# Shorter zero matmuls before the first scores, and moved words, in the opening table of an attention-and-MLP kernel

## The chip, the core and the metric

The kernel runs on one core of a Trainium2 chip. The core has five engines that work at the same time, each through its own list of instructions in order: TensorE (PE; its weight loads, PEld, overlap its matmuls), VectorE (DVE), ScalarE (ACT), GpSimd (POOL) and SyncE (SP). Engines wait for each other through semaphores. Transfers (DMAs) are issued by an engine, here mostly by GpSimd and SyncE, and land later.

The metric is the time of one execution on the device in microseconds (us). Before the change the median of three runs is 321.03 us (321.01 to 321.31).

## What is computed

Causal attention with a forget gate for 8 batches x 8 heads, 576 positions, head size 64, and then a two-layer MLP with a tanh-approximated gelu:

```python
scores = scale * np.matmul(q, k.transpose(0, 1, 3, 2))
cum = np.cumsum(np.log(np.clip(f, 0.0001, 1.0)), axis=-1)
decay = cum[:, :, :, None] - cum[:, :, None, :]
scores = np.where(causal, -1000000000.0, scores + decay)
attn = softmax(scores)
x = np.matmul(attn, v)          # as (4608, 512): tokens x (head, d)
h = x @ w_in                    # 512 -> 2048
g = 0.5 * h * (1.0 + np.tanh(c * (h + 0.044715 * h * h * h)))
out = g @ w_out                 # 2048 -> 512
```

## The kernel before

Attention is worked in 16 quads of four heads. Quad i loads its queries and keys (q_c, k_c), VectorE transposes them into qT and kT, TensorE makes the scores in rounds into PSUM (ps_s), ScalarE takes the exponential into pt, GpSimd or VectorE masks the diagonal blocks, and TensorE multiplies pt with the weighted values vw (line 341 or 355) and with the gate's weights alone for the denominators. VectorE divides and writes xT, the MLP's input. The MLP works in nine chunks of 512 tokens: the first product into ps_h (lines 403 and 439), the gelu on ScalarE into gT, and the second product (lines 619 and, for chunk 0, 692).

Nothing is scheduled by a planner. The order is written by hand in the tables of words FRONT, SECOND, STEADY, FLUSH and LAST. `run` reads a table word by word and emits the instructions of each word; every engine keeps that order in its own list. So moving a word matters for an engine only if it passes another word with instructions on that same engine, or on its queue of transfers.

The words that the change and the prediction touch:

- `B.n.w`: n matmuls of zeros, w columns wide, on TensorE (line 258, `keep_busy`); they wait for nothing but the zeros. `BK.i.n`: n such matmuls of 512 columns that read quad i's transposed keys (line 264).
- `S.i.r`: round r of the scores of quad i, four heads, into two PSUM pairs, followed by two exponentials (lines 285 and 293). `H.i.r.g`: the same for two of the four heads, one pair and one exponential. There are two such pairs (pool psS), handed out in turn, also to `I`, `J` and `v`.
- `M` and `m`: masks by GpSimd (line 299) or by a product with a triangle on VectorE (line 329). `tr`: copies of the triangle into the two tiles `causal`, three copies on ScalarE (lines 740 and 741); `UT` makes the triangle on GpSimd.
- `D`: denominators (line 341 or 355). `V`, `v`: the product with the values, `v` into a pair of psS (ps_o).
- `TK.i`, `TQ.i`: transposes of keys and queries of quad i on VectorE (line 216). `LK.i`, `LQ.i`: their loads, issued by GpSimd (line 209).
- `LP.t`: values of batch 0, a block of 128 positions t, issued by GpSimd; LP.4 is the last block, half as long. `WI.c`, `WO.c`: blocks of the weights w_in and w_out, also issued by GpSimd (lines 198 and 202).
- `CE.n`: the gate's weights, on ScalarE (line 754). `w.0`, `cl`: small copies on ScalarE. `X`: a dummy exponential that has the table loaded ahead.
- `j.0.g.n`, `J.0.g`: n steps, or all, of the first MLP product for half of chunk 0 (line 439), with the gelu behind; `I`: the same for a whole chunk (line 403).
- `F.c.n`: n steps of the second product of chunk c; for chunk 0 (line 692) a step is one matmul of 128 columns of gT against 512 columns. `f.c.n`: the same steps, each as four matmuls of 32 columns side by side.

Of the kernel before, what the change touches and what calls it, by code (L numbers as in the profile page):

```python
# [16 lines left out]
def kernel(  # L17
# [12 lines left out]
    B, H, S, D = q.shape  # L30
# [38 lines left out]
    ON_ACT = ()  # L69

    FRONT = """
        B.1.128 B.1.512 B.1.256 SC B.8.512 B.1.256 B.1.512 B.1.128 LP.0 LP.1 CT B.2.512 WI.1 B.1.256 TK.0 B.1.128 B.1.128 BK.0.2 WI.0 LP.4
        BK.0.1 B.1.512 CE.0 TQ.0 B.1.512 CE.1 LP.3 B.1.512 BK.0.1 S.0.0 B.1.128 B.1.128 LP.2 TK.1 M.0.0 w.0 WI.5 BK.0.1 B.3.512 WI.2 H.0.2.1
        WI.3 B.1.128 TQ.1 BK.0.1 B.1.128 B.1.128 B.1.256 B.1.128 BK.1.1 B.1.512 H.0.1.0 WI.4 D.0.0 vw.0.0 vw.1.0 H.0.2.0 B.2.512 BK.1.1
        B.1.128 H.1.0.1 H.1.0.0 M.1.0 B.1.128 B.1.512 B.1.128 B.1.512 B.1.128 V.0.1.0 H.1.2.0 H.0.1.1 V.0.0.0 H.0.3.0 D.1.0 V.1.1.0 j.0.0.4
        M.0.1 UT LQ.2 WI.7 V.1.0.0 H.0.3.1 H.1.3.1 j.0.0.4 j.0.0.8 H.1.1.0 vw.0.1 WI.6 H.1.1.1 RJ.0.0 M.0.3 D.0.1 LK.2 WO.1 WO.0 j.0.1.8
        VW.1.1 H.1.2.1 tr H.1.3.0 M.1.3 V.0.1.1 V.0.0.1 J.0.2 j.0.1.8 M.1.1 D.1.1 V.1.0.1 V.1.1.1 GJ.0.1 W.1 TQ.2 J.0.3 J.1.1 GJ.0.0 J.1.3
        J.1.0 U.0 WO.2 J.1.2 LK.3 WO.3 LQ.3 LC.1.0 PW.2.1 PW.2.2 F.0.3 LC.1.3 f.0.2 LC.1.4 LC.1.1 LC.1.2 TK.2 f.0.1 LK.4 LQ.4 f.0.1 S.2.0
        F.0.5 TK.3 m.2.0 F.0.5 S.2.2 F.0.2 f.0.5 TQ.3 f.0.2 S.2.1 f.0.3 LV.2.1 F.0.6 S.3.0 F.0.2 m.2.1 vw.2 cl.2 F.0.2 f.0.1 LV.2.0 X M.2.2
        D.2 M.3.0 LQ.5 f.0.1 S.3.1 VW.3 f.0.2 V.2.0 LK.5 TQ.4 TK.4 f.0.4 S.3.2 LV.3.1 LQ.6 f.0.1 m.3.1 f.0.3 LK.6 V.2.1 M.3.2 f.0.3 S.4.1  # L80
        f.0.1 F.0.5 VW.4 TQ.5 F.0.1 X H.4.2.0 H.4.2.1 D.3 f.0.1 cl.3 H.4.0.0 H.4.0.1 V.3.1 v.3.0 vw.5 U.1 f.0.2 m.4.2.2 I.1.2 I.1.1 UW.2.4
        TK.6 I.1.0 CL.5 U.2 m.4.2.3 I.1.3 I.1.5 TQ.6 U.3 TK.5 I.1.4 G.0 I.1.6 M.4.1 I.1.7 F.1.1 G.1.1.2 cl.4 F.1.5 LV.3.0 F.1.5 S.5.0 F.1.5
        M.5.0 F.1.7 m.4.0 F.1.2 UW.2.3 F.1.2 LK.8 F.1.7 LK.7 D.4 S.5.1 F.1.17 LQ.8 F.1.1 S.5.2 M.5.2.3 M.5.2.2 f.1.2 V.4.0 f.1.1 M.5.1 f.1.8
        LQ.7@m.3.1 f.1.1 V.4.1 S.6.0 M.6.0 f.1.4 D.5 f.1.10 S.6.1 f.1.1 M.6.1 f.1.2 V.5.1 vw.6 F.1.4 CL.6 F.1.5 S.6.2 m.6.2.3 V.5.0 f.1.4
        m.6.2.2 f.1.3
    """

    SECOND = """
        Y F.-1.99 T.0.1 T.0.2 LB.2.0 T.0.3 T.0.4 LB.2.1 I.0.0 LB.2.2 E.0.2.2 I.0.1 LB.2.3 TK.3 LK.5 LB.2.4 E.0.2.2 TQ.3 LQ.5 TQ.4 I.0.2 E.0.2.2 I.0.3
        E.0.2.1 TK.4 G.0 VW.3 I.0.6 I.0.7 G.1.1.2 X F.0.13 S.3.0 M.3.0 f.0.9 UW.0.1 D.2 f.0.9 S.3.1 M.3.1 V.2.0 f.0.12 S.3.2 M.3.2 CL.3 V.2.1 VW.4  # L90
        f.0.14 S.4.0 UW.0.2 M.4.0 D.3 f.0.10 V.3.0 UW.0.4 CL.4 UW.0.3 S.4.1 f.0.13 M.4.1 V.3.1 S.4.2 F.0.9 M.4.2 F.0.2 F.0.1
    """

    STEADY = """
        LK.4 LQ.4 Q.0.2 Y LB.2.0 T.0.1 T.0.2 LB.2.1 F.-1.2 Q.0.2 i.0.2.4 T.0.4 LB.2.2 i.0.2.4 T.0.3 Q.0.2 TQ.3 LQ.5 Q.0.2 F.-1.6 i.0.3.4 Q.0.2 Q.0.2
        LB.2.3 TK.3 LB.2.4 LK.5 i.0.3.4 Q.0.2 TK.4 TQ.4 F.-1.99 I.0.6 i.0.7 G.0 S.3.0 X G.1.1.2 f.0.16 M.3.0 D.2 VW.3 f.0.12 S.3.1 M.3.1 V.2.0 f.0.13
        S.3.2 M.3.2 CL.3 V.2.1 VW.4 f.0.15 S.4.0 D.3 f.0.10 V.3.0 M.4.0 CL.4 S.4.1 f.0.14 M.4.1 V.3.1 S.4.2 F.0.12 M.4.2
    """

    FLUSH = """  # L100
# [21 lines left out]
    def many(n, shape, dtype, name):  # L122
        return [singles.tile(shape, dtype, name=f"{name}{i}") for i in range(n)]
# [11 lines left out]
    vw = many(2, [128, NT + 1, 4, D], BF16, "vw")  # L135
# [760 lines left out]
```

## Time and profile before

| | |
|---|---|
| median of the runs | 321.03 us |
| the profiled execution, whole | 321.58 us |
| its span, first to last instruction | 319.9 us |
| TensorE clock granted, mean | 1.0 |
| largest groups on TensorE's side of the chain | second MLP product (line 619) 31%, first (line 403) 19%, scores (line 285) 10% |
| zero matmuls (line 258), share of the chain | 3% |

A timeline row reads: start in us from the span's start, duration, engine, line, operation, tiles written <- read, shape, how many instructions are merged into the row, and in brackets the idle time before the first of them with what ended it. Several instructions in a row overlap at their ends, so the row's duration is from the first start to the last end. A row of the waits reads: who waited <- for whom: us in total, times, longest. A row of a landing gives the time from issue to arrival of the transfer, in us.

### The profile page before, as it was taken

The numbers are of one execution on the slowest core, as the hardware profiler recorded it, in microseconds if no ns is written. First come the engines' busy times: TensorE is split into PE (matmuls) and PEld (weight loads), VectorE is DVE, ScalarE is ACT, GpSimd is POOL, SyncE is SP. The second block draws the span as 40 slices with busy tenths as digits, with TensorE's granted clock in tenths as the row PEclk, the third lists the DMA queues.
The fourth block names the chain that finished last, engine by engine and source line by source line (L and its number), as shares of the span: only waits on it lengthen the run. The fifth ranks groups of instructions, "written<-read, shape, count | busy, mean of one in ns | idle before, by whom it ended". The sixth has DMA issues, their size and how long they took to land.

```text
span 319.9 us, 11741 instructions
## 1 busy us (share of the span) xinstructions
PE 314.1 (98%) x5292; PEld 220.7 (69%) x5311; DVE 243.3 (76%) x368; ACT 213.0 (67%) x248; POOL 108.2 (34%) x146
## 2 busy tenths in 40 slices
PE   8999999999999999999999999999999999999996
PEld 3467834445776567776778877767776786688785
DVE  7675638698978879879877998599886866597674
ACT  3676777866766776878667867787596744836610
POOL 8789625600340416400851065305610150000000
PEclk9999999999999999999999999999999999999999
DMA  7999998951273911594129411971002111010213
GB/s 125 229 199 196 207 234 202 220 150 37 54 130 103 200 22 37 115 209 77 37 75 223 104 39 30 209 160 38 5 33 68 35 33 38 24 43 2 98 35 99
DMA packets 47491, 33.41 MB, mean 104 GB/s; under 512 B 29777, under 2 KB 42193, under 8 KB 47441
## 3 DMA queue, kind: packets, MB, share of 16 engines
q0 software_dynamic: 9632, 15.99, 28.3%
q1 hardware_dynamic: 37664, 16.60, 19.4%
q8 instruction: 41, 0.67, 0.9%
q10 hardware_dynamic: 144, 0.07, 0.1%
q14 instruction: 10, 0.07, 0.1%
HBM read 36.85 MB, written 9.44 MB: 145 GB/s over the span
## 4 chain that ended last, share of the span: by engine, by line
PE 98%; DVE 1%; issue 1%
PE ps_w L619 31%; PE ps_h L403 19%; PE ps_s L285 10%; PE ps_q L539 10%; PE po L355 9%; PE ps_h L439 5%; PE pso L692 4%; PE ps_u L487 4%; PE idle_ps L258 3%; PE po_m L341 2%; PE ps_p L619 1%; PE ps_o L355 0%; PE idle_ps L264 0%; DVE xT L387 0%; PE cum_ps L749 0%
## 5 line engine op out<-in xcount | busy, mean ns | idle before, releaser
L293 ACT ACTIVATE pt<-ps_s 128x1024 bf16<-128x1024 f32 (+2 forms) x100 | 94.0, 991 | 37.5 <-PE ps_s L285 35.9
L299 POOL TENSOR_SCALAR_AFFINE_SELECT pt<-pt 128x512 bf16<-128x512 bf16 (+3 forms) x70 | 43.3, 629 | 108.3 <-ACT pt L293 85.6
L403 PE MATMUL ps_h<-xT,w_in_sb 128*128 128x512 bf16 (+1 forms) x307 | 65.5, 357 | 0.8 <-issue 0.2
L403 PEld LDWEIGHTS <-w_in_sb 128*128 128x128 bf16 x320 | 31.1, 98 | 26.5 <-issue 0.6
L411 ACT ACTIVATE gT<-ps_h 128x1024 bf16<-128x1024 f32 x34 | 34.6, 1018 | 20.3 <-PE ps_h L403 20.1
L619 PEld LDWEIGHTS <-gT 128*32 128x32 bf16 (+1 forms) x1177 | 43.9, 97 | 5.7 <-issue 2.2
L619 PE MATMUL ps_w<-w_out_sb,gT 128*32 128x256 bf16 (+1 forms) x996 | 42.7, 273 | 0.0
L619 PEld LDWEIGHTS <-gsum 128*32 128x32 bf16 (+1 forms) x909 | 35.1, 97 | 3.9 <-issue 1.7
L285 PE MATMUL ps_s<-qT,kT 32*128 32x64 bf16 (+5 forms) x896 | 35.2, 261 | 0.0
L555 DVE TENSOR_TENSOR usnap<-ps_q,usnap 128x1024 f32<-128x1024 f32 x15 | 17.9, 1221 | 17.3 <-PE ps_q L539 12.7
L619 PE MATMUL ps_w<-usum,gsum 128*32 128x256 bf16 (+1 forms) x752 | 29.8, 273 | 0.0
L233 POOL TENSOR_TENSOR vw<-v_nat,wT 128x1280 bf16<-128x1280 f32 (+1 forms) x12 | 27.4, 2279 | 2.7 <-DMA v_nat<-in_v_dram 2.4
L285 PEld LDWEIGHTS <-kT 32*128 32x128 bf16 x896 | 16.2, 92 | 16.8 <-issue 10.2
L636 DVE COPY snap<-ps_w 128x512 f32<-128x512 f32 x32 | 21.8, 682 | 6.5 <-PE ps_w L619 6.3
L550 ACT ACTIVATE gT<-usnap 128x1024 bf16<-128x1024 f32 x15 | 15.8, 1052 | 11.0 <-DVE usnap L555 10.7
L387 DVE TENSOR_TENSOR xT<-po,rb 128x576 bf16<-128x576 f32 x26 | 19.5, 751 | 4.6 <-PE po L355 4.4
L355 PE MATMUL po<-pt,vw 128*32 128x64 bf16 (+4 forms) x624 | 22.6, 278 | 0.0
L355 PEld LDWEIGHTS <-vw 128*32 128x32 bf16 x672 | 14.6, 97 | 9.6 <-issue 3.0
L216 DVE STREAM_TRANSPOSE kT<-k_c 128x576 f32<-128x576 f32 x16 | 19.4, 1244 | 2.1 <-DMA k_c<-in_k_dram 2.1
L216 DVE STREAM_TRANSPOSE qT<-q_c 128x576 f32<-128x576 f32 x16 | 19.8, 1245 | 0.3 <-DMA q_c<-in_q_dram 0.3
L209 POOL DMA_DIRECT2D k_c<-in_k_dram x16 | 9.1, 572 | 29.0 <-DVE kT L216 17.4
L539 PEld LDWEIGHTS <-w_in_sb 128*128 128x128 bf16 x160 | 15.6, 98 | 2.1
(135 smaller groups left out, 489.6 us busy)
## 6 DMA issues: line engine op xcount, KB each, us to landing
out_dram<-o_st SPq DMA_DIRECT2D x35, 256.0 KB, 2.2
k_c<-in_k_dram POOLq DMA_DIRECT2D x16, 288.0 KB, 5.5
q_c<-in_q_dram POOLq DMA_DIRECT2D x16, 288.0 KB, 6.6
v_nat<-in_v_dram SPq DMA_DIRECT2D x16, 256.0 KB, 5.3
v_nat<-in_v_dram SPq DMA_DIRECT2D x20, 128.0 KB, 5.3
v_nat<-in_v_dram POOLq DMA_DIRECT2D x8, 256.0 KB, 10.0
w_in_sb<-in_moe_w_in_dram POOLq DMA_DIRECT2D x8, 256.0 KB, 8.6
w_out_sb<-in_moe_w_out_dram POOLq DMA_DIRECT2D x4, 512.0 KB, 10.6
```

Source lines behind the costliest of these rows:

```text
L216: return nc.vector.transpose(out=dst.rearrange("p s c -> p (s c)").bitcast(FP32) .rearrange("p (t a) -> p a t", a=n), in_=src.rearrange("p ...
L233: return eng.tensor_mul(vw[i % 2][:, t0:t1], vb[:, t0:t1, h0:h0 + 4, :], wT[:, i, t0:t1, :].unsqueeze(3).to_broadcast([128, t1 - t0, 4, D]))
L285: nc.tensor.matmul(tiles[h // 2][:, h % 2, c0:c0 + nq], key_columns(i, key, h, c), qq[32 * h:32 * h + 32, q0:q0 + nq, c], start=(c == 0 an ...
L293: nc.scalar.activation(p[:, 2 * g:2 * g + 2, off:off + n], t[:, :, 0:n], AF.Exp, scale=scale)
L299: nc.gpsimd.affine_select(out=x, in_=x, compare_op=ALU.is_ge, fill=0.0, base=0, pattern=pattern, channel_multiplier=-1)
L355: nc.tensor.matmul(po[r0:r0 + w.shape[-1], 448 + q0:448 + q0 + nq], w, p[:, h, col:col + nq], start=(key in (0, "low")), stop=(key in ("lo ...
L387: nc.vector.tensor_mul(xT[:, 2 * u + x, r0 + s0:r0 + s1], po, rbs[i, part])
L403: nc.tensor.matmul(ph[:, j, n * cols:(n + 1) * cols], w_in_sb[:, dt, 128 * ft:128 * ft + 128], xT[:, dt, h0:h0 + cols], start=(dt == 0 and ...
L411: nc.scalar.activation(gelus(c, 2 * pr, 2), ph, AF.Gelu_apprx_tanh)
L539: nc.tensor.matmul(ps[:, k, HC * n:HC * n + HC], w[:, d, 128 * n:128 * n + 128], x[:, d, :], start=(first and n == 0 and d == 0), stop=(d ...
L619: nc.tensor.matmul(ps[c0:c0 + width, n, cols[0]:cols[1]], x[:, j, 128 * n + c0:128 * n + c0 + width], w[:, j, cols[0]:cols[1]], start=(fir ...
L636: copy(kept[name], ps)
```

## The change

Only the table FRONT changes; in SECOND and STEADY the words stay the same and the lines are wrapped otherwise. The lines of FRONT are wrapped anew as well, so the diff is given by stretches of words:

```diff
- TK.0 B.1.128 B.1.128 BK.0.2 WI.0 LP.4 BK.0.1 B.1.512 CE.0 TQ.0
- B.1.512 CE.1 LP.3 B.1.512 BK.0.1 S.0.0 B.1.128 B.1.128 LP.2 TK.1 M.0.0 w.0
+ TK.0 B.1.128 B.1.128 BK.0.2 LP.4 BK.0.1 B.1.512 WI.0 CE.0 TQ.0
+ BK.0.1 LP.3 B.1.128 B.1.128 CE.1 S.0.0 LP.2 TK.1 M.0.0 w.0
...
- H.1.0.0 M.1.0 B.1.128 B.1.512 B.1.128 B.1.512 B.1.128 V.0.1.0
+ H.1.0.0 B.1.128 B.1.512 B.1.128 B.1.512 M.1.0 B.1.128 V.0.1.0
...
- H.1.2.1 tr H.1.3.0 M.1.3 V.0.1.1 V.0.0.1 J.0.2 j.0.1.8 M.1.1 D.1.1 V.1.0.1
+ H.1.2.1 H.1.3.0 M.1.3 V.0.1.1 V.0.0.1 J.0.2 j.0.1.8 M.1.1 D.1.1 tr V.1.0.1
...
- TK.2 f.0.1 LK.4 LQ.4 f.0.1 S.2.0 F.0.5 TK.3 m.2.0 F.0.5 S.2.2
+ TK.2 LQ.4 f.0.2 S.2.0 F.0.5 TK.3 m.2.0 F.0.4 LK.4 F.0.1 S.2.2
...
- V.2.1 M.3.2 f.0.3 S.4.1 f.0.1 F.0.5 VW.4
+ V.2.1 M.3.2 f.0.4 S.4.1 F.0.5 VW.4
```

What this does to the engines' lists:

- TensorE: ahead of S.0.0 stand one B.1.512 less twice over and two B.1.128 more; behind S.0.0 the two B.1.128 are gone. At S.4.1 one step of f comes before the scores instead of after them. Nothing else moves.
- ScalarE: the three copies of `tr` come behind the last exponential of quad 1, the load of the gelu table and the first gelu.
- GpSimd: LP.4 is issued before WI.0, and LQ.4 before LK.4. Eight semaphores tell of the landings of GpSimd's loads in turn, so a load also waits for the landing of the one eight places before it: the earlier of the two slots of quad 4 waits for LK.3, the later for WO.3, whichever load stands there.
- VectorE and SyncE: the same lists.

More of the change, by code (lines that the diff above doesn't have):

```diff
@@ L71 @@
     FRONT = """
[L72 to L83, printed above, removed]
@@ L84 @@
-        LQ.7@m.3.1 f.1.1 V.4.1 S.6.0 M.6.0 f.1.4 D.5 f.1.10 S.6.1 f.1.1 M.6.1 f.1.2 V.5.1 vw.6 F.1.4 CL.6 F.1.5 S.6.2 m.6.2.3 V.5.0 f.1.4
-        m.6.2.2 f.1.3
+        B.1.128 B.1.512 B.1.256 SC B.8.512 B.1.256 B.1.512 B.1.128 LP.0 LP.1 CT B.2.512 WI.1 B.1.256 TK.0 B.1.128 B.1.128 BK.0.2 LP.4 BK.0.1
+        B.1.512 WI.0 CE.0 TQ.0 BK.0.1 LP.3 B.1.128 B.1.128 CE.1 S.0.0 LP.2 TK.1 M.0.0 w.0 WI.5 BK.0.1 B.3.512 WI.2 H.0.2.1 WI.3 B.1.128 TQ.1
+        BK.0.1 B.1.128 B.1.128 B.1.256 B.1.128 BK.1.1 B.1.512 H.0.1.0 WI.4 D.0.0 vw.0.0 vw.1.0 H.0.2.0 B.2.512 BK.1.1 B.1.128 H.1.0.1
@@ new lines @@
+        H.1.0.0 B.1.128 B.1.512 B.1.128 B.1.512 M.1.0 B.1.128 V.0.1.0 H.1.2.0 H.0.1.1 V.0.0.0 H.0.3.0 D.1.0 V.1.1.0 j.0.0.4 M.0.1 UT LQ.2
+        WI.7 V.1.0.0 H.0.3.1 H.1.3.1 j.0.0.4 j.0.0.8 H.1.1.0 vw.0.1 WI.6 H.1.1.1 RJ.0.0 M.0.3 D.0.1 LK.2 WO.1 WO.0 j.0.1.8 VW.1.1 H.1.2.1
+        H.1.3.0 M.1.3 V.0.1.1 V.0.0.1 J.0.2 j.0.1.8 M.1.1 D.1.1 tr V.1.0.1 V.1.1.1 GJ.0.1 W.1 TQ.2 J.0.3 J.1.1 GJ.0.0 J.1.3 J.1.0 U.0 WO.2
+        J.1.2 LK.3 WO.3 LQ.3 LC.1.0 PW.2.1 PW.2.2 F.0.3 LC.1.3 f.0.2 LC.1.4 LC.1.1 LC.1.2 TK.2 LQ.4 f.0.2 S.2.0 F.0.5 TK.3 m.2.0 F.0.4 LK.4
@@ new lines @@
+        F.0.1 S.2.2 F.0.2 f.0.5 TQ.3 f.0.2 S.2.1 f.0.3 LV.2.1 F.0.6 S.3.0 F.0.2 m.2.1 vw.2 cl.2 F.0.2 f.0.1 LV.2.0 X M.2.2 D.2 M.3.0 LQ.5
+        f.0.1 S.3.1 VW.3 f.0.2 V.2.0 LK.5 TQ.4 TK.4 f.0.4 S.3.2 LV.3.1 LQ.6 f.0.1 m.3.1 f.0.3 LK.6 V.2.1 M.3.2 f.0.4 S.4.1 F.0.5 VW.4 TQ.5
+        F.0.1 X H.4.2.0 H.4.2.1 D.3 f.0.1 cl.3 H.4.0.0 H.4.0.1 V.3.1 v.3.0 vw.5 U.1 f.0.2 m.4.2.2 I.1.2 I.1.1 UW.2.4 TK.6 I.1.0 CL.5 U.2
+        m.4.2.3 I.1.3 I.1.5 TQ.6 U.3 TK.5 I.1.4 G.0 I.1.6 M.4.1 I.1.7 F.1.1 G.1.1.2 cl.4 F.1.5 LV.3.0 F.1.5 S.5.0 F.1.5 M.5.0 F.1.7 m.4.0
@@ L86 @@
+        F.1.2 UW.2.3 F.1.2 LK.8 F.1.7 LK.7 D.4 S.5.1 F.1.17 LQ.8 F.1.1 S.5.2 M.5.2.3 M.5.2.2 f.1.2 V.4.0 f.1.1 M.5.1 f.1.8 LQ.7@m.3.1 f.1.1
+        V.4.1 S.6.0 M.6.0 f.1.4 D.5 f.1.10 S.6.1 f.1.1 M.6.1 f.1.2 V.5.1 vw.6 F.1.4 CL.6 F.1.5 S.6.2 m.6.2.3 V.5.0 f.1.4 m.6.2.2 f.1.3
     """
     SECOND = """
-        Y F.-1.99 T.0.1 T.0.2 LB.2.0 T.0.3 T.0.4 LB.2.1 I.0.0 LB.2.2 E.0.2.2 I.0.1 LB.2.3 TK.3 LK.5 LB.2.4 E.0.2.2 TQ.3 LQ.5 TQ.4 I.0.2 E.0.2.2 I.0.3
-        E.0.2.1 TK.4 G.0 VW.3 I.0.6 I.0.7 G.1.1.2 X F.0.13 S.3.0 M.3.0 f.0.9 UW.0.1 D.2 f.0.9 S.3.1 M.3.1 V.2.0 f.0.12 S.3.2 M.3.2 CL.3 V.2.1 VW.4
@@ L91 @@
-        f.0.14 S.4.0 UW.0.2 M.4.0 D.3 f.0.10 V.3.0 UW.0.4 CL.4 UW.0.3 S.4.1 f.0.13 M.4.1 V.3.1 S.4.2 F.0.9 M.4.2 F.0.2 F.0.1
+        Y F.-1.99 T.0.1 T.0.2 LB.2.0 T.0.3 T.0.4 LB.2.1 I.0.0 LB.2.2 E.0.2.2 I.0.1 LB.2.3 TK.3 LK.5 LB.2.4 E.0.2.2 TQ.3 LQ.5 TQ.4 I.0.2
+        E.0.2.2 I.0.3 E.0.2.1 TK.4 G.0 VW.3 I.0.6 I.0.7 G.1.1.2 X F.0.13 S.3.0 M.3.0 f.0.9 UW.0.1 D.2 f.0.9 S.3.1 M.3.1 V.2.0 f.0.12 S.3.2
+        M.3.2 CL.3 V.2.1 VW.4 f.0.14 S.4.0 UW.0.2 M.4.0 D.3 f.0.10 V.3.0 UW.0.4 CL.4 UW.0.3 S.4.1 f.0.13 M.4.1 V.3.1 S.4.2 F.0.9 M.4.2 F.0.2
@@ L92 @@
+        F.0.1
     """
     STEADY = """
-        LK.4 LQ.4 Q.0.2 Y LB.2.0 T.0.1 T.0.2 LB.2.1 F.-1.2 Q.0.2 i.0.2.4 T.0.4 LB.2.2 i.0.2.4 T.0.3 Q.0.2 TQ.3 LQ.5 Q.0.2 F.-1.6 i.0.3.4 Q.0.2 Q.0.2
-        LB.2.3 TK.3 LB.2.4 LK.5 i.0.3.4 Q.0.2 TK.4 TQ.4 F.-1.99 I.0.6 i.0.7 G.0 S.3.0 X G.1.1.2 f.0.16 M.3.0 D.2 VW.3 f.0.12 S.3.1 M.3.1 V.2.0 f.0.13
-        S.3.2 M.3.2 CL.3 V.2.1 VW.4 f.0.15 S.4.0 D.3 f.0.10 V.3.0 M.4.0 CL.4 S.4.1 f.0.14 M.4.1 V.3.1 S.4.2 F.0.12 M.4.2
+        LK.4 LQ.4 Q.0.2 Y LB.2.0 T.0.1 T.0.2 LB.2.1 F.-1.2 Q.0.2 i.0.2.4 T.0.4 LB.2.2 i.0.2.4 T.0.3 Q.0.2 TQ.3 LQ.5 Q.0.2 F.-1.6 i.0.3.4
@@ L98 @@
+        Q.0.2 Q.0.2 LB.2.3 TK.3 LB.2.4 LK.5 i.0.3.4 Q.0.2 TK.4 TQ.4 F.-1.99 I.0.6 i.0.7 G.0 S.3.0 X G.1.1.2 f.0.16 M.3.0 D.2 VW.3 f.0.12
+        S.3.1 M.3.1 V.2.0 f.0.13 S.3.2 M.3.2 CL.3 V.2.1 VW.4 f.0.15 S.4.0 D.3 f.0.10 V.3.0 M.4.0 CL.4 S.4.1 f.0.14 M.4.1 V.3.1 S.4.2 F.0.12
+        M.4.2
     """
```

## The prediction

> **What bounds the kernel now.** I read the busy shares and the chain of work that ended last first, then the list of what TensorE waited for, then the timeline of the two stretches that the change touches, with the landings of the loads beside it.
>
> ```profile
> PE 314.1 (98%) x5292; PEld 220.7 (69%) x5311; DVE 243.3 (76%) x368; ACT 213.0 (67%) x248; POOL 108.2 (34%) x146
> ...
> PEclk9999999999999999999999999999999999999999
> ...
> PE 98%; DVE 1%; issue 1%
> ...
> PE idle_ps L258 <- DVE idle L712: 1.3, 1, 1.3
> PE pso L692 <- issue: 0.3, 2, 0.2
> ```
>
> TensorE is busy for 98% of the span, it is 98% of the last chain, and after its first matmul (1.3 us, when the tile of zeros is ready) its longest wait in total is 0.3 us. So the time is the length of TensorE's own list. What shortens that list shortens the kernel, if no engine or load then becomes late; work moved on another engine is worth nothing by itself. A busy TensorE can still hide short waits, because the ends of matmuls are modelled; I look for these by start times.
>
> **The front, up to the first scores.** The words are those of the table FRONT.
>
> ```profile
> 7.24 1.22 DVE L216 STREAM_TRANSPOSE qT<-q_c 128x576 f32<-128x576 f32 x1
> 8.31 0.81 PE L258 MATMUL idle_ps<-idle 128*128 128x512 bf16 x3
> 8.96 0.38 PE L264 MATMUL idle_ps<-kT,idle 128*128 128x512 bf16 x1
> 9.27 0.52 PE L285 MATMUL ps_s<-qT,kT 32*128 32x256 bf16 x16
> 9.83 1.51 ACT L293 ACTIVATE pt<-ps_s 128x768 bf16<-128x768 f32 x2 [1.76 <-PE ps_s L285]
> 10.81 0.46 PE L285 MATMUL ps_s<-qT,kT 32*128 32x320 bf16 x4
> 11.42 1.23 POOL L299 TENSOR_SCALAR_AFFINE_SELECT pt<-pt 128x512 bf16<-128x512 bf16 x2 [0.68 <-ACT pt L293]
> 12.84 0.35 PE L341 MATMUL po_m<-pt,w_bf 128*32 128x256 bf16 x8
> ```
>
> Three 512-column zero matmuls start at 8.31 and the next follows at 8.96, so one costs 0.65 / 3 = 0.216 us; a 128-column one is taken at a quarter, 0.054 (an estimate). S.0.0 needs the transposed queries, ready at 7.24 + 1.22 = 8.46, but starts at 9.27, right behind the zero matmuls: TensorE's order holds it, not the data. The change takes out two 512s ahead of S.0.0 (-0.43) and brings two 128s there from behind it (+0.11). S.0.0 then starts at 8.95, still 0.49 after its queries, so the whole 0.32 is real.
>
> Behind S.0.0 the list is shorter by the two 128s, so the next scores, H.0.2.1, can come 0.43 earlier, at 10.38. They take the PSUM pair that the first exponential frees: that one starts at 9.83 - 0.32 = 9.51 and takes half of 1.51, so it ends near 10.27. It is ready. D.0.0 at 12.84 reads the two masks that GpSimd ends at 12.65; these come 0.32 earlier (12.33) and TensorE 0.43 earlier (12.41). So from there on everything is 0.43 us earlier. Bounds: 0.32, if the exponentials set the pace, to 0.43; nothing at all if the queries are late. I take 0.43, as both covers hold by 0.08 us or more.
>
> **Loads do not move with TensorE.** They stand in one long queue, so their landings stay where they are and eat into the gain.
>
> ```profile
> 7.45 1.61 POOL L186 DMA_DIRECT2D v_nat<-in_v_dram  x2
> DMA to landing us min/median/max: 9.2/9.2/9.2
> 18.20 0.61 PE L439 MATMUL ps_h<-xT,w_in_sb 128*128 128x256 bf16 x4
> ...
> 13.32 0.72 POOL L198 DMA_DIRECT2D w_in_sb<-in_moe_w_in_dram  x1
> w_in_sb<-in_moe_w_in_dram POOLq DMA_DIRECT2D x1, 256.0 KB, 9.0
> 22.78 0.28 PE L439 MATMUL ps_h<-xT,w_in_sb 128*128 128x256 bf16 x1
> ```
>
> WI.0 changes places with the short load LP.4, which was issued at 7.45 and landed 9.2 later, at 16.6. The pair is done by then in either order; j.0.0.4, the first reader of WI.0, comes at 18.20 - 0.43 = 17.77. Cost 0, and 1.1 us of cover. The tightest is WI.2, issued at 13.32 and landing at 22.3: j.0.1.8 starts at 22.78 and would start at 22.35. The gain just fits; were the landing 0.1 later, TensorE would lose about that much. M.1.0 and CE.1 are written elsewhere in the table but keep their place in GpSimd's and ScalarE's lists: 0.
>
> **The triangles.** Three copies on ScalarE move from ahead of quad 1's last exponential to behind it, the table load and one gelu.
>
> ```profile
> 24.86 0.49 ACT L740 CAST causal<-utri_f 128x128 bf16<-128x128 f32 x2
> 25.49 2.79 PE L439 MATMUL ps_h<-xT,w_in_sb 128*128 128x256 bf16 x24
> 25.65 0.81 ACT L293 ACTIVATE pt<-ps_s 128x768 bf16<-128x768 f32 x1
> 26.53 1.60 POOL L299 TENSOR_SCALAR_AFFINE_SELECT pt<-pt 128x512 bf16<-128x512 bf16 x3 [0.41 <-ACT pt L293]
> 27.77 1.94 ACT L432 ACTIVATE gT<-ps_h 128x1024 bf16<-128x1024 f32 x2
> 32.14 1.02 ACT L432 ACTIVATE gT<-ps_h 128x1024 bf16<-128x1024 f32 x1 [2.43 <-PE ps_h L439]
> ```
>
> They fill 24.86 to 25.65, so that exponential comes up to 0.79 earlier, and the masks behind it up to their idle 0.41. Their reader, D.1.1, stands behind the 24 matmuls that keep TensorE until 28.28, and the masks end at 28.13: it does not wait for them, so the gain is 0. The second gelu ends at most 0.79 later than 29.71, at 30.5; ScalarE then still stands idle until 32.14. Without that idle time (2.43 us) the price would be the 0.79. Taken: 0 and no bound beside it, since the cover is three times the price.
>
> **Queries of quad 4 loaded ahead of its keys.** LQ.4 takes the earlier slot and LK.4 the later.
>
> ```profile
> 39.76 0.56 POOL L209 DMA_DIRECT2D k_c<-in_k_dram  x1 [0.78 <-DMA k_c<-in_k_dram]
> 42.05 0.54 POOL L209 DMA_DIRECT2D q_c<-in_q_dram  x1 [1.74 <-DMA w_out_sb<-in_moe_w_out_dram]
> 46.27 1.23 POOL L299 TENSOR_SCALAR_AFFINE_SELECT pt<-pt 128x512 bf16<-128x512 bf16 x2 [3.68 <-ACT pt L293]
> 54.41 1.25 DVE L216 STREAM_TRANSPOSE qT<-q_c 128x576 f32<-128x576 f32 x1
> ```
>
> The second slot waits for a landing either way; behind it GpSimd has only the masks at 46.27, with 3.68 us idle before them. VectorE transposes the queries at 54.41 and the keys after them, over 12 us from the later issue. Cost 0. The words f.0.1 and F.0.5 around S.2.0 are split otherwise but sum to the same list.
>
> **One step of the output product ahead of S.4.1.** Here a step (four 32-column matmuls side by side) moves from behind S.4.1 to before it.
>
> ```profile
> 57.97 0.40 PE L692 MATMUL pso<-w_out_sb,gT 128*32 128x512 bf16 x4
> 58.13 1.94 ACT L293 ACTIVATE pt<-ps_s 128x1024 bf16<-128x1024 f32 x2 [1.06 <-PE ps_s L285]
> 59.70 1.05 PE L285 MATMUL ps_s<-qT,kT 32*128 32x320 bf16 x16
> 60.42 1.94 ACT L293 ACTIVATE pt<-ps_s 128x1024 bf16<-128x1024 f32 x2 [0.28 <-PE ps_s L285]
> 60.68 0.87 PE L355 MATMUL po<-pt,w_bf 128*32 128x512 bf16 x24
> 61.70 1.41 PE L285 MATMUL ps_s<-qT,kT 32*128 32x64 bf16 x24
> 62.81 1.94 ACT L293 ACTIVATE pt<-ps_s 128x1024 bf16<-128x1024 f32 x2
> 63.03 0.86 PE L355 MATMUL po<-pt,vw 128*32 128x512 bf16 x24
> 63.89 0.87 PE L355 MATMUL ps_o<-pt,vw 128*32 128x512 bf16 x24
> ```
>
> From 57.97 to 59.70 TensorE does this step and six full-width ones: 7 x 0.216 = 1.51, and 0.22 is left for two changes of tile shape, 0.11 each. With the step moved, one change goes. Yet S.4.1 and its exponentials come 0.22 later, and H.4.2.1, the second half of the 16 matmuls at 59.70, takes the PSUM pair that the second of them frees (60.07, then 60.29); this half sets D.3, which goes from 60.68 to 60.90. What ends the stretch, however, is ScalarE: v.3.0 at 63.89 takes the pair freed by the exponential that starts at 62.81 and takes 1.02 (the gelu row's time for this size), at 63.83. These exponentials run end to end from 60.42, released by H.4.2.0 at 59.70, which now comes 0.11 earlier. ScalarE is through with S.4.1 at 60.29 and can start at 60.31, so the chain and v.3.0 move by -0.11. D.3's lateness is taken up inside the 24 matmuls at 61.70 (H.4.0.0, H.4.0.1): the second half waits for the exponential that ends at 60.42 + 1.94 = 62.36, and from there to V.3.1 at 63.03, less 0.11 for the change of shape, it takes 0.5. The first half takes as long, so it was done at 62.2 and TensorE stood 0.2 us. Starting at 61.92, the halves end at 62.92, V.3.1 comes at 63.04 and v.3.0 can follow at 63.75 (0.7 for 24 matmuls, an estimate: the 0.87 of the row at 60.68 holds the last one's tail), just ahead of 63.78. Bounds -0.11 and +0.22; I take -0.11, as the rows give the chain end to end.
>
> **Sum:** -0.43 - 0.11 = -0.54 us. Against the profiled execution's own 321.58 us (span 319.9 and 1.7 around it) that gives 321.04; this execution was 0.55 above the median of the runs shown, 321.03, so the forecast for the median is 320.49, said as 320.5.
>
> **Rivals.** *Slow zero matmuls.* Early on the same matmuls took twice as long:
>
> ```profile
> 3.26 0.15 PEld L258 LDWEIGHTS <-idle 128*128 128x128 bf16 x1 [0.28 <-issue]
> 3.69 0.15 PEld L258 LDWEIGHTS <-idle 128*128 128x128 bf16 x1 [0.28 <-issue]
> ```
>
> The weight loads of 512-column matmuls are 0.43 apart there, while the clock row says full speed throughout. If in other executions the slow stretch reaches past 8 us, the two removed cost 0.86 and the time is 321.03 - 0.86 - 0.11 = 320.06. Against it: in this one they are fast by 8.31. [...]
>
> *The step is not taken up.* The 0.22 of D.3 stays on the path: 321.03 - 0.43 + 0.22 = 320.82. For it: the margin by which v.3.0 fits is 0.03.
>
> *The front gains nothing,* as S.0.0 waits for something else: 321.03 - 0.11 = 320.92. Against it: 0.81 us between the queries and S.0.0.
>
> *Slower: the clock falls at the first scores.* There are fewer zeros to keep TensorE busy; if the queries come after the last zero matmul (now 8.86, 0.40 after them), it stands idle, and from an idle TensorE on the slow stretch may return. At the start it ran from 1.26 to some 5.4 (an estimate, from the fast spacing that follows), 4.1 us; once more that is 2.05 us of lost work: 320.49 + 2.05 = 322.5. It decides only from a real gap on, and this trace has none there. [...]
>
> **How the numbers follow.** Forecast 0.55, spread 320.25 to 320.75; slow zeros 0.14; step not taken up 0.12; front worth nothing 0.07; slower 0.12, more than the rows bear out, because margins of 0.03 to 0.08 us were read off one execution. 0.2% is 0.64 us (about what a measurement of this kernel tells from no change), which lies 0.1 beyond the sum, inside the forecast's spread: I count 0.25 of its 0.55 as beyond. Faster 0.14 + 0.25 = 0.39, same 0.30 + 0.12 + 0.07 = 0.49, slower 0.12. The range 320.0 to 321.2 leaves out the slow clock and little else.
>
> **What would show it.** Right: S.0.0 at 8.95, D.0.0 at 12.4, the 24 matmuls at 25.06, copies of the triangles behind the first gelu, v.3.0 at 63.35, and no TensorE wait that was not there. Wrong: j.0.1.8 still near 22.8 (a load holds it), D.3 and v.3.0 both late against the 24 matmuls (the step costs), or 512-column matmuls 0.43 apart after 9 us.

## The result and the profile after

The changed kernel takes 320.48 us (median of 14 runs, 320.35 to 320.70) against 321.05 (14 runs, 320.94 to 322.0): 0.57 us less, a ratio of 0.9981 (95% interval 0.9973 to 0.9988). Predicted were 320.5 us. A second set of runs of both, the control below, gave 320.68 against 321.19, ratio 0.9979 (0.9970 to 0.9989).

The profiled execution of the changed kernel took 320.43 us (span 318.7); that of the kernel before 321.58 (319.9). That is 1.15 less, twice the difference of the medians, so the two traces hold things that are not the change. All line numbers of the changed kernel are one higher (L285 is now L286). First its busy shares, then what TensorE waited for (who waited <- for whom: us in total, times, longest):

```profile
PE 313.0 (98%) x5290; PEld 220.3 (69%) x5309; DVE 246.0 (77%) x368; ACT 212.9 (67%) x248; POOL 109.6 (34%) x146
```

```profile
PE idle_ps L259 <- DVE idle L713: 1.3, 1, 1.3
PE pso L693 <- issue: 0.3, 2, 0.2
...
```

TensorE is as full as before and has no large wait that it didn't have. So the gain must be found by start times. Timeline of the front, TensorE's start-up of the kernel before:

```profile
6.38 0.69 PE L749 MATMUL cum_ps<-ident_f,f_all 64*128 64x64 f32 x5
7.00 0.83 PE L258 MATMUL idle_ps<-idle 128*128 128x512 bf16 x5
```

and of the changed kernel, up to D.0.0:

```profile
6.33 0.48 PE L750 MATMUL cum_ps<-ident_f,f_all 64*128 64x64 f32 x5
...
6.74 0.83 PE L259 MATMUL idle_ps<-idle 128*128 128x512 bf16 x5
...
7.25 1.25 DVE L217 STREAM_TRANSPOSE qT<-q_c 128x576 f32<-128x576 f32 x1
...
8.05 0.38 PE L259 MATMUL idle_ps<-idle 128*128 128x512 bf16 x1
...
8.48 0.28 PE L259 MATMUL idle_ps<-idle 128*128 128x128 bf16 x2
...
8.69 0.52 PE L286 MATMUL ps_s<-qT,kT 32*128 32x256 bf16 x16
...
10.84 1.23 POOL L300 TENSOR_SCALAR_AFFINE_SELECT pt<-pt 128x512 bf16<-128x512 bf16 x2
...
12.14 0.35 PE L342 MATMUL po_m<-pt,w_bf 128*32 128x256 bf16 x8
```

The five small gate matmuls take 0.69 us before and 0.48 after, and the zeros behind them start at 7.00 and 6.74: TensorE went over to its fast rate a little earlier in the second execution (the gate matmuls start 0.11 us apart before and 0.06 after; the record of the granted clock begins, with full speed, at 6.87 us before and at 6.18 after). That is 0.26 us ahead of every changed word. S.0.0 then starts at 8.69 instead of 9.27 (0.58 = 0.26 + 0.32) and D.0.0 at 12.14 instead of 12.84 (0.70 = 0.26 + 0.43, to the rounding). The 0.70 stays constant through the MLP of chunk 0.

The loads of w_in and the triangles' stretch:

```profile
12.02 2.15 POOL L199 DMA_DIRECT2D w_in_sb<-in_moe_w_in_dram  x3
...
22.08 1.05 PE L440 MATMUL ps_h<-xT,w_in_sb 128*128 128x256 bf16 x8
...
24.79 2.79 PE L440 MATMUL ps_h<-xT,w_in_sb 128*128 128x256 bf16 x24
...
25.33 1.63 POOL L300 TENSOR_SCALAR_AFFINE_SELECT pt<-pt 128x512 bf16<-128x512 bf16 x3
26.75 1.02 ACT L433 ACTIVATE gT<-ps_h 128x1024 bf16<-128x1024 f32 x1 [0.48 <-PE ps_h L440]
...
27.67 0.49 ACT L741 CAST causal<-utri_f 128x128 bf16<-128x128 f32 x2
...
28.45 1.02 ACT L433 ACTIVATE gT<-ps_h 128x1024 bf16<-128x1024 f32 x1
...
31.44 1.02 ACT L433 ACTIVATE gT<-ps_h 128x1024 bf16<-128x1024 f32 x1 [1.96 <-PE ps_h L440]
```

WI.2, the second of the three loads, is issued at 12.74 instead of 13.32 and lands at 21.25 instead of 22.3; j.0.1.8 starts at 22.08 (0.70 earlier, like all the rest). The copies stand behind the first gelu, the masks come 1.2 earlier (25.33 instead of 26.53), the second gelu at 28.45 and the third at 31.44, which is 0.70 earlier again.

Last, the stretch of S.4.1 on TensorE and ScalarE:

```profile
56.87 0.63 PE L286 MATMUL ps_s<-qT,kT 32*128 32x64 bf16 x16
...
57.60 1.94 ACT L294 ACTIVATE pt<-ps_s 128x1024 bf16<-128x1024 f32 x2 [1.21 <-PE ps_s L286]
...
58.84 1.38 PE L286 MATMUL ps_s<-qT,kT 32*128 32x320 bf16 x16
...
59.56 1.94 ACT L294 ACTIVATE pt<-ps_s 128x1024 bf16<-128x1024 f32 x2
...
60.14 0.87 PE L356 MATMUL po<-pt,w_bf 128*32 128x512 bf16 x24
...
61.95 1.94 ACT L294 ACTIVATE pt<-ps_s 128x1024 bf16<-128x1024 f32 x2
...
63.02 0.87 PE L356 MATMUL ps_o<-pt,vw 128*32 128x512 bf16 x24
```

S.4.1 starts at 56.87 and its two exponentials at 57.60, so that ScalarE has them behind it at 59.54, just before the next, which starts at 59.56 (60.42 before) and is followed by H.4.0's at 61.95. H.4.2.0 starts at 58.84 instead of 59.70, 0.86 earlier; D.3 at 60.14 instead of 60.68, only 0.54 earlier; and v.3.0 at 63.02 instead of 63.89, 0.87 earlier. D.3 is late against its neighbours, v.3.0 isn't.

The last piece of the 1.15 is, of these two traces, only in that of the kernel before: a row whose 24 matmuls take 1.12 us where others of the shape take 0.85 to 0.87. Inside it no matmul starts between 94.63 and 94.89:

```profile
94.19 1.12 PE L355 MATMUL po<-pt,vw 128*32 128x512 bf16 x24
```

Together: 0.26 (start-up) + 0.43 (front) + 0.06 (a step of 0.05 to 0.06 at 54.5 us) + 0.12 (S.4.1) + 0.27 (this hole) = 1.14. The front and S.4.1, 0.55, are the change as predicted. Start-up and hole, 0.53, are differences of two executions (the control below shows the hole in the changed kernel too); they are about the 0.55 by which this profiled execution of the kernel before lay above its median.

### The profile page after: what moved, and what is told of

It is laid out like the page before. It is cut to its first block, busy times and chain, and to the rows that moved or that the text cites. A ratio compares the mean times of both kernels' runs of the same rounds, so it can differ in the third digit from the quotient of the medians.

```text
span 318.7 us, 11738 instructions
## 1 busy us (share of the span) xinstructions
PE 313.0 (98%) x5290; PEld 220.3 (69%) x5309; DVE 246.0 (77%) x368; ACT 212.9 (67%) x248; POOL 109.6 (34%) x146
## 4 chain that ended last, share of the span: by engine, by line
PE 97%; issue 1%; DVE 0%; ACT 0%
PE ps_w L620 31%; PE ps_h L404 19%; PE ps_s L286 10%; PE ps_q L540 10%; PE po L356 9%; PE ps_h L440 5%; PE pso L693 4%; PE ps_u L488 4%; PE idle_ps L259 3%; PE po_m L342 2%; PE idle_ps L265 1%; PE ps_p L620 1%; PE ps_o L356 0%; ACT pt L294 0%; DVE xT L388 0%
## 5 line engine op out<-in xcount | busy, mean ns | idle before, releaser
L300 POOL TENSOR_SCALAR_AFFINE_SELECT pt<-pt 128x512 bf16<-128x512 bf16 (+3 forms) x70 | 44.3, 645 | 99.1 <-ACT pt L294 76.3
L286 PE MATMUL ps_s<-qT,kT 32*128 32x64 bf16 (+5 forms) x896 | 35.1, 261 | 0.1
L286 PEld LDWEIGHTS <-kT 32*128 32x128 bf16 x896 | 16.1, 92 | 16.5 <-issue 10.8
```

Source lines behind the costliest of these rows:

```text
L286: nc.tensor.matmul(tiles[h // 2][:, h % 2, c0:c0 + nq], key_columns(i, key, h, c), qq[32 * h:32 * h + 32, q0:q0 + nq, c], start=(c == 0 an ...
L300: nc.gpsimd.affine_select(out=x, in_=x, compare_op=ALU.is_ge, fill=0.0, base=0, pattern=pattern, channel_multiplier=-1)
```

## The experiments

All times are medians of the runs of one set, each beside the kernel before in the same set. "Landing" is the landing of the queries of quad 0, which S.0.0 needs transposed.

**The front's zero matmuls alone, in two sets of runs.**

```diff
- BK.0.1 B.1.512 CE.0 TQ.0 B.1.512 CE.1 LP.3 B.1.512 BK.0.1 S.0.0 B.1.128 B.1.128 LP.2
+ BK.0.1 B.1.512 CE.0 TQ.0 BK.0.1 LP.3 B.1.128 B.1.128 CE.1 S.0.0 LP.2
```

> The kernel before with the front's zero matmuls alone: two of 512 columns less ahead of the first scores, the two of 128 columns from behind them to ahead of them; no other word moved. Theory: these two 512s are worth their own length, 2 x 0.216 = 0.43 us, so 320.6 against 321.05, and the 24 matmuls of line 439 that started at 25.49 start 0.43 earlier (give or take 0.26 for the start-up, which differed by that much between the two profiles). Rival, the loads hold the gain: nothing of it left at 25 us, 321.0. Rival, these matmuls ran at half speed: -0.86, 320.2.

Measured: 321.00 us (320.64 to 322.19) against 321.06, ratio 1.0001 (0.9991 to 1.0012). The lowest is where the theory wants it, the median is not. The profiled execution was one of the long ones, 321.92 us:

```profile
8.64 1.25 DVE L216 STREAM_TRANSPOSE qT<-q_c 128x576 f32<-128x576 f32 x1 [1.31 <-DMA q_c<-in_q_dram]
...
9.95 0.52 PE L285 MATMUL ps_s<-qT,kT 32*128 32x256 bf16 x16 [1.19 <-DVE qT L216]
```

The queries landed at 8.62 us (7.05 and 7.23 in the two traces above), although issued at the same 2.02. VectorE stood 1.31 us for them and TensorE 1.19. S.0.0 starts 1.26 later than in the changed kernel, and the execution is 1.28 above the lowest of its set: that is nearly all of the difference. TensorE's rate held through this gap: S.0.0 takes 0.52 us as in the changed kernel, and from 10.63 to 39 us all starts keep the same distance from those of the kernel before. Two theories were left for the late landing: the order of the loads behind it (WI.0 ahead of LP.4) makes it late (A), or it varies by itself (B). The next four ran as one set against each other, on another chip (11) than this set and the later ones (7).

> The front alone once more (the same words as in the run that gave 321.0 us). Theory A: 320.9 to 321.1 again, with late queries in part of the executions. Theory B: as the control plus the 0.11 of the step, whatever the control shows; a median of 320.6 here would say that the first 321.0 was the chip of that run.

Measured: 320.70 (320.59 to 321.09) against 321.19, ratio 0.9982 (0.9973 to 0.9991), landing 7.36. With the same words as in the first set the 0.43 is there. So the 321.00 was not the words. The chip alone doesn't explain it: on chip 7 the queries landed at 6.94 to 7.49 us in the seven other profiles, and the kernel with three more zeros left out (below) gave 320.58. Only one execution of that first set was profiled, so what made the others long is not shown.

**The changed kernel again; WI.0 and LP.4 exchanged back in it; the exchange added to the front.**

```diff
# changed kernel, exchanged back
- LP.4 BK.0.1 B.1.512 WI.0 CE.0
+ WI.0 LP.4 BK.0.1 B.1.512 CE.0
# front alone, exchange added
- WI.0 LP.4 BK.0.1 B.1.512 CE.0
+ LP.4 BK.0.1 B.1.512 WI.0 CE.0
```

> The kernel after the change once more, as the control on the same chip as the next three. Theory A (the exchange of WI.0 and LP.4 lets the first queries land early and steadily): 320.5 again, its times within 0.35 of each other, queries of quad 0 landing near 7.2. Theory B (the landing of these queries varies by itself, and any kernel with the shorter front meets it): some of its executions 0.5 to 1.4 above the fastest, median up to 321.0.

> The kernel after the change with WI.0 issued before LP.4 again, and nothing else. Theory A: like the front alone, median near 320.9 with executions up to 1.5 above the fastest. Theory B, the exchange is worth nothing: the same median and spread as the control.

> The kernel before with the front's zero matmuls and the exchange of WI.0 and LP.4, no other word moved. Theory A: the 0.43 us of the zeros is there, 320.62, with little spread. Theory B: the same as the front alone, 320.6 at best and a median up to 321.0.

Measured against 321.19: the control 320.68 (320.44 to 321.00); exchanged back 320.85 (320.34 to 321.41), ratio 0.9986 (0.9978 to 0.9995); front with the exchange 320.75 (320.59 to 321.63), ratio 0.9989 (0.9979 to 0.9998). All intervals overlap. Of the two front kernels the one with the exchange has the wider spread, of the two changed kernels the one without it: theory A is not borne out. The control's profiled execution (320.98) shows the small form of the same wait:

```profile
7.61 1.26 DVE L217 STREAM_TRANSPOSE qT<-q_c 128x576 f32<-128x576 f32 x1 [0.16 <-DMA q_c<-in_q_dram]
...
8.92 0.52 PE L286 MATMUL ps_s<-qT,kT 32*128 32x256 bf16 x16
...
93.56 1.16 PE L356 MATMUL po<-pt,vw 128*32 128x512 bf16 x24
```

Landing at 7.58, transposed at 8.87, S.0.0 at 8.92 instead of 8.69. This 0.23 is less than half of the 0.55 by which the execution is longer than the one profiled first. The other 0.31 is a hole like that of the kernel before, in the last row: no matmul starts between 94.01 and 94.43 us. The same kernel has it in one execution and not in the other, so the changed words don't decide it. In the 14 profiles of this study the landing lies between 6.94 and 7.68, and once at 8.62. In the changed kernel a landing up to about 7.4 is free (8.69 less the transposition's 1.25 and 0.05 until TensorE starts); four of the 14 are later. In the kernel before it was free up to 7.97; one of the 14 is later.

**The step ahead of S.4.1 alone.**

```diff
- f.0.3 S.4.1 f.0.1 F.0.5 VW.4
+ f.0.4 S.4.1 F.0.5 VW.4
```

> The kernel before with one step of the output product ahead of S.4.1 instead of behind it, and nothing else. Theory: one change of tile shape less, -0.11 us from H.4.2.0 on (60.42 for the exponential it releases), D.3 0.22 - 0.11 or more late but the stretch ending with v.3.0 0.11 earlier than 63.89, so 320.94 against 321.05. Rival, the lateness of D.3 and of the second pair of exponentials stays on the path: v.3.0 0.22 later, 321.27.

Measured: 321.17 (320.84 to 321.61) against 321.06, ratio 1.0001 (0.9992 to 1.0010). An effect of 0.11 us can't be seen in these times, so the trace has to tell. It began 0.10 late (from the start-up, constant from 8 to 57 us), and then:

```profile
60.41 1.94 ACT L293 ACTIVATE pt<-ps_s 128x1024 bf16<-128x1024 f32 x2
...
60.99 0.87 PE L355 MATMUL po<-pt,w_bf 128*32 128x512 bf16 x24
...
63.02 0.87 PE L355 MATMUL po<-pt,vw 128*32 128x512 bf16 x24
63.88 0.84 PE L355 MATMUL ps_o<-pt,vw 128*32 128x512 bf16 x20
```

Before they were 60.42, 60.68, 63.03 and 63.89. Less the 0.10, D.3 is 0.21 later and the exponential and v.3.0 are 0.11 earlier. The theory's numbers, place by place.

**A second step ahead of S.4.1, in the changed kernel.**

```diff
- f.0.4 S.4.1 F.0.5
+ f.0.5 S.4.1 F.0.4
```

> The kernel after the change with a second step of the output product ahead of S.4.1. No change of tile shape is saved this time. Theory (ScalarE's exponentials end the stretch, with 0.02 us between the end of S.4.1's exponentials and the start of the next): S.4.1 0.22 later, the next exponential 0.2 later than 59.56 and v.3.0 with it: +0.2 us, 320.8 against the changed kernel's 320.6. Rival, TensorE's own list ends the stretch and the 0.2 us wait ahead of H.4.0.1 takes it up: 0, v.3.0 where it was.

Measured: 320.89 (320.45 to 321.12) against 321.04, ratio 0.9992 (0.9983 to 1.0000), which leaves 0.15 of the change's 0.51 to 0.57 (the changed kernel itself was not in this set). The trace (0.28 late from its start-up):

```profile
60.01 1.90 ACT L294 ACTIVATE pt<-ps_s 128x1024 bf16<-128x1024 f32 x2
60.08 0.62 PE L286 MATMUL ps_s<-qT,kT 32*128 32x320 bf16 x8 [0.28 <-ACT pt L294]
...
63.45 0.87 PE L356 MATMUL ps_o<-pt,vw 128*32 128x512 bf16 x24
```

The exponential starts 0.45 later than the changed kernel's 59.56 and v.3.0 0.43 later than 63.02; less 0.28, 0.17 and 0.15. The theory said 0.2: one step is free, the second isn't, because ScalarE's chain has no room left.

**What was costed at nothing: copies and both exchanges of loads, in the kernel before.**

```diff
- H.1.2.1 tr H.1.3.0
+ H.1.2.1 H.1.3.0
- D.1.1 V.1.0.1
+ D.1.1 tr V.1.0.1
- LK.4 LQ.4 f.0.1 S.2.0 F.0.5 TK.3 m.2.0 F.0.5 S.2.2
+ LQ.4 f.0.1 S.2.0 F.0.5 TK.3 m.2.0 F.0.4 LK.4 F.0.1 S.2.2
- WI.0 LP.4 BK.0.1 B.1.512 CE.0
+ LP.4 BK.0.1 B.1.512 WI.0 CE.0
```

> The kernel before with the parts that were costed at nothing, together: the triangle copies behind quad 1's last exponential and first gelu, WI.0 and LP.4 exchanged, LQ.4 ahead of LK.4. Theory: 0, 321.05, TensorE's starts from 25 us to the end unchanged within 0.05 apart from a difference of the start-up. Rival: the later landing of the last block of quad 4's values (65.2 instead of 61.0 in the two profiles) comes from these exchanges and costs up to 0.2 somewhere behind 66 us.

Measured: 321.07 (320.93 to 321.79) against 321.06, ratio 1.0003 (0.9994 to 1.0012). TensorE's starts are later than in the kernel before by a constant 0.05 us up to 54.5 us, which is the start-up, and equal from there on. This gain of 0.05 us at S.3.2 is in the changed kernel's trace too, and not in that of the front alone, of the step alone or of the front with WI.0 and LP.4 exchanged. So it belongs to the copies or to the exchange of quad 4's loads; what makes it wasn't found. The last block of quad 4's values, which landed late in the changed kernel (65.2 us instead of 61.0), costs nothing and isn't theirs either: in the front alone, in its second set, it lands at 64.8.

**The copies five times over, in the changed kernel** (tr five times in place of once).

> The kernel after the change with the triangle copies made five times over, to use up the cover that they were costed against. Theory: four more sets of 0.79 put the second gelu 3.1 us later, which is 1.2 more than ScalarE's idle time before the third gelu (1.96); the group of the first MLP product that takes the PSUM pair of the second gelu then waits about that long: +1.2 to +1.4 us, 321.9. Rival, TensorE doesn't need that pair so soon: 0, 320.6.

Measured: 321.37 (320.98 to 321.74) against 321.04, ratio 1.0009 (1.0000 to 1.0017). The trace (0.31 late before this place):

```profile
31.95 2.85 ACT L433 ACTIVATE gT<-ps_h 128x1024 bf16<-128x1024 f32 x3
...
33.94 2.23 PE L440 MATMUL ps_h<-xT,w_in_sb 128*128 128x256 bf16 x19 [0.48 <-ACT gT L433]
```

The second gelu starts at 31.95 instead of 28.45; less the 0.31 that is 3.2 us later, against 3.1 worked out. The group that starts at 32.98 in the changed kernel comes at 33.94: 0.96, less 0.31, 0.65 instead of the 1.2 to 1.4. The mechanism is right; what the estimate left out is that the third gelu used to end at 32.46, half a us before TensorE needed its pair (1.2 - 0.5 = 0.7). The copies have 1.96 + 0.5 us of cover behind their own place.

**No zero matmuls from TQ.0 up to V.0.1.0, in the changed kernel.** This leaves out zeros only, no part of what is computed: 24 matmuls, together 16 times one of 512 columns, so 3.5 us at 0.216 each (the 26 words and 5 us below are too many).

> The kernel after the change without any zero matmul from the transposes of quad 0's queries (TQ.0) up to V.0.1.0: 26 words of zeros, on average some 5 us of TensorE's work, left out. Theory: the zeros stand where TensorE would wait for exponentials, masks and values anyway; only those still ahead of S.0.0 can be worth something, queries being ready at 8.50 and S.0.0 starting at 8.69: about -0.15 and S.0.0 near 8.55, 320.3 against 320.48 of the changed kernel. Rival, the clock falls when TensorE stands idle: the following matmuls of full width 0.43 apart again for up to 4 us, +2 us, 322.4. Rival, zeros behind S.0.0 hold the order up too: down to 320.0.

Measured: 325.52 (325.0 to 325.93) against 321.06, ratio 1.0135 (1.0121 to 1.0149). The page's clock row (40 slices of the span, tenths of full speed), what TensorE waited for, and one row of its timeline:

```profile
PEclk9859999999999999999999999999999999999999
```

```profile
PE ps_s L286 <- ACT pt L294: 1.6, 3, 0.9
PE po L356 <- issue: 1.4, 1, 1.4
...
PE po_m L342 <- POOL pt L300: 0.7, 2, 0.4
```

```profile
21.05 2.69 PE L440 MATMUL ps_h<-xT,w_in_sb 128*128 128x256 bf16 x12
```

The granted clock falls to 0.8 and 0.5 in the slices from 8 to 24 us, and its mean over the execution is 0.984. The 12 matmuls at 21.05 stand 0.21 us apart; in the changed kernel such matmuls are 0.11 apart (the eight at 22.08). Where TensorE was kept waiting for data, S.0.0 and D.0.0 did come earlier (0.20 and 0.54), but by 24 us the half rate has cost 3.1 us against the changed kernel. Another 1.6 comes of a single wait for nothing that the profile shows ("issue"), with no matmul started between 93.69 and 95.50 us.

**Only the zeros between S.0.0 and D.0.0 left out, in the changed kernel.** They are 8.5 times one of 512 columns, 1.84 us and so about half of those above.

> The kernel after the change without the zero matmuls between S.0.0 and D.0.0 (1.73 us of them), those before and behind left in. Theory: D.0.0 is held by GpSimd's masks (ready at 12.06, D.0.0 at 12.15), so at best -0.1, and TensorE stands idle there for about half of 3.2 us. If half is enough to lose the clock, as in the run without all zeros, matmuls at half rate for some 10 us: +3 us, 323.6. If it is not: 320.5 to 320.6, the same as the changed kernel.

Measured: 324.81 (322.12 to 326.26) against 321.04, ratio 1.0106 (1.0074 to 1.0138).

```profile
10.17 0.46 PE L286 MATMUL ps_s<-qT,kT 32*128 32x320 bf16 x4 [0.90 <-ACT pt L294]
10.87 0.63 PE L286 MATMUL ps_s<-qT,kT 32*128 32x320 bf16 x8 [0.24 <-ACT pt L294]
...
12.21 0.28 PE L342 MATMUL po_m<-pt,w_bf 128*1 128x128 bf16 x4 [0.29 <-POOL pt L300]
...
13.47 0.63 PE L259 MATMUL idle_ps<-idle 128*128 128x512 bf16 x1 [0.33 <-issue]
13.89 0.63 PE L265 MATMUL idle_ps<-kT,idle 128*128 128x512 bf16 x1
...
93.71 0.40 PE L620 MATMUL ps_w<-usum,gsum 128*32 128x256 bf16 x8 [2.00 <-issue]
...
95.05 2.34 PE L620 MATMUL ps_w<-usum,gsum 128*32 128x256 bf16 x40
```

Up to 12.2 us TensorE has waited 0.90, 0.24 and 0.29. Behind that the 512-column matmuls at 13.47 and 13.89 start 0.42 apart (0.22 in the changed kernel, at 12.81), and TensorE, level with the changed kernel at 12.42 (12.43 there), is 1.21 us behind it at 18.72 (17.51 there). Most of the rest of this execution's 5.0 above the changed kernel is the wait of 2.0 us ahead of 93.71 and a second slow stretch behind it: the 40 matmuls at 95.05 take 2.34 us, and 1.26 in the changed kernel (at 91.23). Five of the six executions have a mean clock of 0.988 to 0.995; the sixth, the shortest (322.12), has 1.0, so the clock did not fall in it, and what made it 1.6 longer than the changed kernel is not shown. In five of six, leaving out half of the zeros is already too much.

**The last three zeros ahead of S.0.0 left out, in the changed kernel.**

```diff
- BK.0.1 LP.3 B.1.128 B.1.128 CE.1 S.0.0
+ LP.3 CE.1 S.0.0
```

> The kernel after the change without the last three zero matmuls ahead of S.0.0 (one of 512 columns, two of 128), so that only the queries of quad 0 hold S.0.0. Theory: S.0.0 starts as soon as they are transposed, near 8.55 where they land early (-0.15) and where it did in the other executions; median 320.5 against 320.6, lowest 320.2. Rival, the idle time before S.0.0 is enough to lose the clock: +2 us or more.

Measured: 320.58 (320.30 to 321.08) against 321.04, ratio 0.9986 (0.9977 to 0.9994).

```profile
7.42 1.26 DVE L217 STREAM_TRANSPOSE qT<-q_c 128x576 f32<-128x576 f32 x1 [0.24 <-DMA q_c<-in_q_dram]
...
8.73 0.52 PE L286 MATMUL ps_s<-qT,kT 32*128 32x256 bf16 x16 [0.45 <-DVE qT L217]
```

S.0.0 starts 0.05 behind the transposed queries, and the clock stays (mean granted 1.0, S.0.0 in 0.52 us behind a wait of 0.45). The lowest time is 0.05 lower than the changed kernel's lowest in its first set; the median isn't. There is no measurable gain left here, since the queries now decide. None of the kernels tried is shown to beat the changed one.

## Why the prediction was right, point by point

- **Two 512-column zeros are worth 0.43.** Shown: 0.43 of the traces' 0.70 at D.0.0, and the front alone 0.49 below the kernel before in its second set (0.06 in its first, whose profiled execution had late queries). Predicted as 8.95, S.0.0 came at 8.69; the 0.26 is the start-up. So are the differences at D.0.0 (12.4 predicted, 12.14) and at the 24 matmuls (25.06, 24.79); v.3.0 (63.35, 63.02) has the 0.06 of 54.5 us besides.
- **"Still 0.49 after its queries."** Mis-sized: 0.18 (queries transposed at 8.51, S.0.0 at 8.69), because the faster start-up moved the zeros (from 7.00 to 6.74) and not the landing (7.05 and 7.23). With the landing's spread this is the one place where the change loses in part of its executions. The rival "the front gains nothing, as S.0.0 waits for something else" was given as a case for the whole kernel; the runs show it as an event, total in one profiled execution of the front alone and 0.23 in one of the changed kernel.
- **"Loads do not move with TensorE."** Wrong, harmlessly. GpSimd issues them behind its masks, the masks follow the exponentials, and these follow S.0.0: the masks started at 10.84 instead of 11.42, WI.2 was issued 0.58 earlier and landed 1.05 earlier. The margin predicted at 0.05 us was 0.83 (21.25 to 22.08) in this execution. It is not always so wide: in the seven other profiles with the shorter front, leaving out the one with the very late queries and the two with many zeros less, the load took 8.4 to 9.5 us and the margin was 0.12 to 0.98. No wait for this load was seen, but the prediction was nearly right that the gain only just fits. So this queue didn't stand still against TensorE, as GpSimd, which issues it, was held by TensorE's results.
- **Triangles and exchanged loads at 0.** In the times shown (1.0003, 0.9994 to 1.0012); the trace has a gain of 0.05 without a cause. The cover of the copies was larger than stated: besides ScalarE's idle time TensorE had half a us of its own.
- **One step, -0.11.** Not in the times (the step alone gave 321.17 against 321.06), but in two traces: D.3 is 0.33 late against its neighbours and v.3.0 isn't; the margin, predicted at 0.03, shows in the second step's cost of 0.15 to 0.17. The rival "the step is not taken up" falls.
- **Slow zero matmuls.** The end of the slow stretch differs between the two profiles of the result: the record of the granted clock begins, with full speed, at 6.87 us in the kernel before and at 6.18 in the changed one. In the front alone (both sets), the control and the kernel with the last three zeros less, the gate matmuls, from 6.18 to 6.33 on, take 0.48 to 0.49 us as in the changed kernel. The stretch did not reach the removed zeros at 8.31 in the kernel before, which ran at 0.216 each. The prediction's end of the slow stretch, 5.4 us, was misread: in the kernel before a 512-column zero still takes 0.42 us at 5.61, and the stretch lasts to 6.87 us, 5.6 us from 1.26, so the price of the slow clock would have been 2.8 us and not 2.05 (an estimate, half of the 5.6).
- **The clock falls at the first scores.** It did not, and not only for want of a gap: in the front alone the late queries made the gap that this rival asks for, 1.19 us, and the rate held (S.0.0 in 0.52 us). That the clock can fall was shown by leaving out more: without the zeros between S.0.0 and D.0.0, three waits of 0.90, 0.24 and 0.29 us went before the 512-column matmuls that start 0.42 apart. So the length of the longest gap does not decide it in these two runs; where the limit lies, they don't show.

The sum came out right also because the two errors, on the cover of the queries and on the loads, had no price in most executions: that is luck, as far as the margins of single traces go. The forecast of -0.54 compares with -0.57 and -0.51 in the two sets.

## What to carry to other kernels

Filler matmuls ahead of a data-bound start are worth their length only down to the latest usual landing of that data, so compare several executions' landings, not one, before taking the last of them out. Filler in front of waits was worth keeping here, although every wait in the front without it was shorter than one us (0.90 the longest): without it the mean granted clock of the profiled executions was 0.988 and 0.984, and the medians rose by 3.8 and 4.5 us. When two profiles differ by more than their medians do, match the starts instruction by instruction and take out the steps that stand ahead of, or far from, every changed word.

## What the runs showed of the hardware

- The same load, issued at the same time (2.02 us), landed 4.9 to 6.6 us later (queries of quad 0, 14 profiles: 6.94 to 7.68, and 8.62).
- Behind waits of 0.90, 0.24 and 0.29 us, up to 12.2 us, TensorE's 512-column matmuls started 0.42 apart instead of 0.22 (half of the zeros left out, mean granted clock 0.988). With none of the zeros from TQ.0 up to V.0.1.0 the clock was at 0.8 and 0.5 in the slices from 8 to 24 us (mean 0.984), and 256-column matmuls started 0.21 apart instead of 0.11. One gap of 1.19 us, in the front alone, did not slow it.
- TensorE stood still for nothing that the profile names, near 92 to 95 us: 0.26 to 0.42 us between two starts in the profiles of the kernel before, of the step alone and of the control, and 1.4 to 2.0 us in the two with most zeros left out. The instruction queue of the changed kernel (page, DMA queues: packets, MB, share) moved 41 packets, 0.67 MB, so 16 KB each:

```profile
q8 instruction: 41, 0.67, 0.9%
```

In the kernel before one such packet starts at 92.68 us, ahead of the end of its wait, and TensorE goes on at 94.89, 2.21 us behind it. In the changed kernel one starts at 90.62, and the matmul that stands in the same place starts at 93.77, 3.15 us behind it, without a wait. Whether the packet has to do with the wait was not tried.
